# Another order of relu, finish and spectra steps in the final stage, and one prefetch load a unit earlier

## Chip, core and metric

The kernel runs on one core of a Trainium2 chip. The metric is the device time of one execution in microseconds (us); lower is better. The kernel before took 461.34 us, the median of 8 runs (459.61 to 462.4).

PE is TensorE, ACT or ScalarE the activation engine, DVE or VectorE the vector engine, POOL or GpSimd the general engine, SP or SyncE the queue that issues most DMAs. Each works through its own queue in program order and waits on semaphores. PE writes its results to PSUM; GpSimd's adds here read and write SBUF alone.

## What is computed

Sliding-window attention with a bias that falls with distance makes x; then the first 64 Fourier modes of x along the sequence are multiplied by complex weight matrices, one pair per mode, transformed back and added to x; the sum goes through one dense layer with a relu.

```
q, k, v: 8 batches x 8 heads x 576 tokens x 64     x = attention, 8 x 576 x 512
X = rfft(x, axis=1)[:, :64]
Yr = Xr @ w_r - Xi @ w_i;  Yi = Xr @ w_i + Xi @ w_r      (per mode, 512 x 512 float32)
y = irfft(Y, n=576)
u = x + y
out = u + max(u @ w_ch, 0)
```

## The kernel before

**Attention.** Sixteen units, one for each batch and each half of the heads, go through a software pipeline. Its order is written out by hand in `STAGE` (step name, tile, lag in units). The order of instructions on every engine, SP among them, is that of the program: no scheduler moves any. `norm` (L348) writes a unit's x; SP loads q, k and v two units ahead (L208 to L220).

**Weights.** There are 128 weight matrices of 512 x 512 float32, 1 MB each. `load_w` fetches one either by SP (L453, kept as float32, the upper halves used as bf16) or by GpSimd (L449, the DMA converts to bf16). During attention, GpSimd fetches the first ones into the 14 buffers of pool `early`. The table `AHEAD` says after which pipeline stage how many loads are issued: `13: 4` means four after stage 13. Ahead of them GpSimd copies one element of the x of unit stage-1 into a gate tile (L520). This holds the load back until that unit is normalized. `LATER` adds three loads after each of stages 14 and 15. After attention, eight more GpSimd loads reuse early buffers, and SP streams the others through six, later eight, float32 buffers.

**Weight stage.** For each group of four modes, L648 multiplies the spectra XC with the weights into `acc`. Beside it, `early_spectra` and `project` prepare what the first 32 modes and x give: `project` leaves x @ w_ch and the first half of the modes' share of it in `XW` (L629). After the last group, `quad_end` moves the result into YT (L541 to L553), and the final stage starts.

**Final stage.** The output is cut into 18 units j: units 0 to 3 are the four token tiles of batches 0 and 1, 4 to 7 those of batches 2 and 3, 8 the last 64 tokens of these four batches; 9 to 12, 13 to 16 and 17 are the same for batches 4 to 7. Four pairs of batches bp need a spectra step each.

- `spectra(1, bp, ...)`, called for bp = 0 directly and by `late_spectra` (steps s1 to s3) for the others: four L566 matmuls give zw, four L569 matmuls give z, into a yy buffer; ACT copies zw to `ZW` (L571); z goes to `Z` in two copies (L573), on ACT for s1 to s3 and on DVE for bp = 0.
- `activate(j)` (step a): L712 matmuls bring XW into an mm buffer, L587 matmuls add the second half of the modes from ZW, ACT writes the relu to r (L731). For j in `POOLED`, GpSimd then adds x to r (L733).
- `finish(j)` (step f): for j not in `POOLED`, two L739 matmuls bring x into a yy buffer; L752 matmuls (L758 for units 8 and 17) add y = FT.T @ Z; DVE adds yy and r into o (L766); SP writes o out (L768, or L776 for units 8 and 17).

mm and yy have two PSUM buffers each, r has four buffers in SBUF, o five. A unit's mm is free when its relu is done, its yy when DVE's add is done, a spectra step's yy when its copies are done. The order of steps is a string written out by hand:

```python
        begin(0)
        add_tokens(0)
        spectra(1, 0, pair("yy")[:, 0], pair("mm")[:, 0], nc.vector.tensor_copy)
        for step in ("a0 f0 a1 a2 f1 s1 a3 a4 f2 f3 a5 a6 f4 f5 s2 a7 a8 f6 f7 a9 a10 f8 f9 s3 "
                     "a11 a12 f10 f11 a13 a14 f12 f13 a15 a16 f14 f15 a17 f16 f17").split():
```

`add_tokens(0)` ahead of the loop takes the first yy buffer for unit 0, and f0 gives it back.

Of the kernel before, what the change touches and what calls it, by code (L numbers as in the profile page):

```python
# [397 lines left out]
def kernel(  # L398
# [10 lines left out]
    nc = tc.nc  # L409
    ctx.enter_context(tc.manual_schedule(engines=ALL | {SP}))  # L410
    B, H, S, _ = q.shape
    NM, DM, _ = moe_w_r.shape
    AHEAD = {0: 1, 1: 1, 2: 1, 4: 1, 5: 1, 7: 1, 8: 1, 10: 1, 11: 1, 13: 4, 14: 1}
    LATER = {14: 3, 15: 3}
    EARLY, NWA, NWB, AGAIN = 14, 6, 2, 8
    HM = NM // 2
# [23 lines left out]
    def load_w(n, pool, bf16, chosen=None):  # L440


        for i in ([i for i in todo_w if i not in again][:n] if chosen is None else chosen):
            todo_w.remove(i)
            src = (moe_w_r, moe_w_i)[i % 2][i // 2].rearrange("(p a) e -> p a e", a=4)
            homes[i] = pool
            if bf16:
                t = spare.pop(0) if pool is None else pool.tile([P, 4, DM], BF16, tag="w", name="w")
                nc.gpsimd.dma_start(out=t, in_=src)  # L449
                wq[i] = [t[:, a] for a in range(4)]  # L450
            else:
                t = pool.tile([P, 4, DM], FP32, tag="w", name="w")
                nc.sync.dma_start(out=t, in_=src)  # L453
                wq[i] = [t[:, a].bitcast(BF16)[:, 1::2] for a in range(4)]

    with ExitStack() as actx:
# [51 lines left out]
        for stage in range(min(lags), n + max(lags)):  # L508
# [6 lines left out]
            if stage == 3:  # L515
                at.inverse_table()
            if stage in AHEAD:
                if stage:
                    b, g = at.units[stage - 1]
                    nc.gpsimd.tensor_copy(gate[:1, :1], x[:1, b, 0, 256 * g : 256 * g + 1])  # L520
                load_w(AHEAD[stage], early, True)
            if stage in LATER:
                load_w(LATER[stage], None, True)

    with ExitStack() as mctx:
# [35 lines left out]
        def spectra(hf, bp, zw, z, copy):  # L561

            lhsT = [YT[:, hf, et, 2 * bp : 2 * bp + 2].rearrange("p b r m -> p (b r m)")
                    for et in range(4)]
            for et in range(4):
                nc.tensor.matmul(zw, lhsT=lhsT[et], rhs=wch[:, et],  # L566
                                 start=(et == 0), stop=(et == 3))
            for et in range(4):
                nc.tensor.matmul(z[:, et * P : (et + 1) * P], lhsT=lhsT[et], rhs=ident,  # L569
                                 start=True, stop=True)  # L570
            nc.scalar.copy(ZW[:, bp, hf], zw)  # L571
            for i in range(2):
                copy(Z[ROWS[i], 2 * bp + (i if hf else 1 - i)], z[ROWS[i]])  # L573
# [24 lines left out]
        def token_tiles(j):  # L598
            b, st = units[j]
            return x[:, b : b + 2, st] if st < FULL else x[:, b + 1 : b + 4 : 2, FULL]  # L600
# [91 lines left out]
        pctx.close()  # L692
        wctx.close()

        fin = mctx.enter_context(tc.tile_pool(name="res", bufs=4, reuse_waits="tile"))
        ps = mctx.enter_context(
            tc.tile_pool(name="tps", bufs=2, space=PSUM, reuse_waits="tile")
        )
        POOLED = (2, 4, 6, 8, 10, 12, 14)
        mms, yys, rs = {}, {}, {}  # L700

        def pair(tag):
            return ps.tile([P, 2, DM], FP32, tag=tag, name=tag)
# [13 lines left out]
        def activate(j):  # L717
# [12 lines left out]
            for part in ((slice(0, 1), slice(1, 2)) if j == 0 else (slice(0, 2),)):  # L730
                nc.scalar.activation(r[:, part], mm[:, part], AF.Relu)  # L731
            if j in POOLED:
                nc.gpsimd.tensor_tensor(out=r, in0=r, in1=token_tiles(j), op=ALU.add)  # L733
# [8 lines left out]
        def finish(j):  # L742

            b, st = units[j]
            if j in POOLED:
                yys[j] = pair("yy")
# [3 lines left out]
            for n in range(2):  # L750
                if st < FULL:
                    nc.tensor.matmul(  # L752
                        yy[:, n], lhsT=FT[:, n, st * P : (st + 1) * P], rhs=Z[:, b + n],
                        start=j in POOLED, stop=True, skip_group_check=True,
                    )
                    continue
                for half in range(2):
                    nc.tensor.matmul(  # L758
                        yy[ROWS[half], n], lhsT=FT[:, half, FULL * P :],
                        rhs=Z[:, b + half + 2 * n],  # L760
                        start=j in POOLED, stop=True, skip_group_check=True,
                    )
# [17 lines left out]

        def late_spectra(bp):
            zz = pair("yy")
            spectra(1, bp, zz[:, 0], zz[:, 1], nc.scalar.copy)

        begin(0)
        add_tokens(0)
        spectra(1, 0, pair("yy")[:, 0], pair("mm")[:, 0], nc.vector.tensor_copy)
        for step in ("a0 f0 a1 a2 f1 s1 a3 a4 f2 f3 a5 a6 f4 f5 s2 a7 a8 f6 f7 a9 a10 f8 f9 s3 "
                     "a11 a12 f10 f11 a13 a14 f12 f13 a15 a16 f14 f15 a17 f16 f17").split():
            {"a": activate, "f": finish, "s": late_spectra}[step[0]](int(step[1:]))  # L790


# [28 lines left out]
```

## Time and profile before

| | us |
|---|---|
| median of 8 runs | 461.34 |
| the profiled execution, its own time | 461.3 |
| its span, first to last instruction | 459.2 |
| last weight matmul (L648) starts | 415.28 |
| first DVE add of the final stage (L766) starts | 420.74 |
| last DVE add ends | 454.32 |

Busy in the whole span: PE 363.1 us, DVE 171.8, ACT 155.5, POOL 51.8. From 418.8 to 454.4 us, most of the final stage: PE 27.7 us, DVE 22.9, ACT 22.6, POOL 14.8 of 35.6.

The page divides the span into forty slices with one digit of busy share for each engine; DMA there is the mean share of sixteen DMA engines, which can pass 1 by a little in the finer windows. In rows of instructions the first two numbers are the start in us and the length in us, x4 counts merged instructions, and square brackets tell how long the engine sat idle before and what ended it. In the chain of waits, "issue" is time in which nothing visible was waited for.

### The profile page before, as it was taken

How to read it: one execution, taken by the hardware profiler on the slowest of the kernel's cores; microseconds unless marked ns; L12 is line 12 of the kernel's file. 1: busy time of each engine (PE TensorE's matmuls, PEld its weight loads, DVE VectorE, ACT ScalarE, POOL GpSimd, SP SyncE). 2: the span in 40 equal slices, each digit the busy share in tenths (PEclk: the TensorE clock that was granted, in tenths of full speed). 3: DMA queues.
4: the chain of work that ended last, by engine and by line, in shares of the span. 5: the costliest groups of instructions: out<-in, count | busy, mean ns of one | idle time of the engine just before them, and what ended most of it. 6: DMA issues, size and time to landing. Idle time of an engine off the chain costs nothing. (4 is left out here: it accounts for less than half of the span.)

```text
span 459.2 us, 7797 instructions
## 1 busy us (share of the span) xinstructions
PE 363.1 (79%) x3271; PEld 191.2 (42%) x3294; DVE 171.8 (37%) x312; ACT 155.5 (34%) x193; POOL 51.8 (11%) x84
## 2 busy tenths in 40 slices
PE   5797999999875558656676798998989788988773
PEld 4466777777653222212222243443433333433331
DVE  7988799998722001000010142111111211203555
ACT  6878899999700000000000021211111111104761
POOL 8510101002310100000000000000000000001460
PEclk9999899999989575776666699999999999999998
DMA  8999999996999999999999999999999999991687
GB/s 284 323 338 308 291 292 307 329 289 179 214 310 317 281 314 317 345 398 425 417 422 422 422 420 420 418 422 420 420 420 422 418 420 420 421 378 49 230 274 274
DMA packets 51875, 158.31 MB, mean 345 GB/s; under 512 B 3713, under 2 KB 22657, under 8 KB 39041
## 3 DMA queue, kind: packets, MB, share of 16 engines
q1 hardware_dynamic: 47280, 142.62, 80.5%
q0 software_dynamic: 4560, 15.21, 16.7%
q8 instruction: 25, 0.41, 0.4%
q14 instruction: 10, 0.07, 0.0%
HBM read 163.58 MB, written 9.44 MB: 377 GB/s over the span
## 5 line engine op out<-in xcount | busy, mean ns | idle before, releaser
L648 PE MATMUL acc<-w,XC 128*32 128x512 bf16 x488 | 147.1, 458 | 50.2 <-DMA w<-in_moe_w_r_dram 27.2
L648 PEld LDWEIGHTS <-XC 128*32 128x32 bf16 x512 | 59.7, 140 | 130.6 <-issue 100.7
L295 ACT ACTIVATE att<-sc 128x1024 bf16<-128x1024 f32 x64 | 64.0, 1031 | 7.8 <-PE sc L285 7.8
L629 ACT CAST XW<-my 128x512 bf16<-128x512 f32 x36 | 21.1, 586 | 109.0 <-PE my L587 109.0
L571 ACT CAST ZW<-zw 128x512 bf16<-128x512 f32 x4 | 2.3, 586 | 138.6 <-PE zw L566 138.6
L543 DVE TENSOR_SCALAR yq<-acc 128x512 bf16<-128x512 f32 x14 | 9.7, 690 | 100.8 <-PE acc L648 100.8
L611 DVE COPY xT<-tr 128x1024 bf16<-128x1024 bf16 x18 | 12.5, 692 | 89.4 <-PE tr L609 89.4
L733 POOL TENSOR_TENSOR r<-r,x 128x1024 f32<-128x1024 f32 x7 | 14.8, 2129 | 273.3 <-ACT r L731 273.3
L332 PE MATMUL av<-vb,att 128*128 128x132 bf16 (+1 forms) x576 | 38.5, 217 | 4.7 <-DVE x L348 3.0
L332 PEld LDWEIGHTS <-att 128*128 128x128 bf16 x704 | 36.6, 98 | 10.3 <-DVE x L348 7.3
L623 PE MATMUL my<-wch,xT 128*64 128x512 bf16 x288 | 37.9, 385 | 0.8 <-DVE xT L611 0.8
L257 ACT COPY qkT<-tp 128x1152 bf16<-128x1152 bf16 x30 | 33.5, 1117 | 3.4 <-PE tp L251 2.6
L285 PE MATMUL sc<-qkT 64*64 64x256 bf16 (+2 forms) x640 | 25.9, 271 | 5.1 <-ACT qkT L257 1.2
L348 DVE TENSOR_TENSOR x<-av,rec 128x640 bf16<-128x640 f32 x32 | 26.4, 825 | 1.1
L766 DVE TENSOR_TENSOR o<-yy,r 128x1024 f32<-128x1024 f32 (+1 forms) x20 | 21.5, 1114 | 12.6 <-POOL r L733 6.6
L285 PEld LDWEIGHTS <-qkT 64*64 64x64 bf16 x640 | 14.9, 111 | 19.9 <-issue 16.9
L623 PEld LDWEIGHTS <-xT 128*64 128x64 bf16 x288 | 13.2, 109 | 22.6 <-issue 9.4
L234 DVE CAST vb<-vr 64x1024 bf16<-64x1024 f32 x32 | 22.2, 694 | 0.2
L306 DVE TENSOR_TENSOR att<-att,mask 128x1024 bf16<-128x1024 bf16 x32 | 20.6, 684 | 0.0
L731 ACT ACTIVATE r<-mm 128x1024 f32<-128x1024 f32 (+1 forms) x19 | 17.3, 981 | 4.0 <-PE mm L587 3.9
L272 PE MATMUL sc<-bias,ident 128*128 128x512 bf16 x48 | 17.1, 413 | 1.4 <-ACT att L295 1.4
L251 PE MATMUL tp<-ident,q 128*128 128x128 bf16 x144 | 12.0, 236 | 4.1 <-DVE q L239 4.1
(104 smaller groups left out, 329.8 us busy)
## 6 DMA issues: line engine op xcount, KB each, us to landing
w<-in_moe_w_i_dram SPq DMA_DIRECT2D x54, 1024.0 KB, 18.4
w<-in_moe_w_r_dram SPq DMA_DIRECT2D x46, 1024.0 KB, 18.5
qr<-in_q_dram SPq DMA_DIRECT2D x16, 576.0 KB, 9.0
kr<-in_k_dram SPq DMA_DIRECT2D x16, 576.0 KB, 8.2
vr<-in_v_dram SPq DMA_DIRECT2D x32, 256.0 KB, 7.2
w<-in_moe_w_r_dram POOLq DMA_DIRECT2D x15, 512.0 KB, 24.5
out_dram<-o SPq DMA_DIRECT2D x15, 512.0 KB, 3.1
w<-in_moe_w_i_dram POOLq DMA_DIRECT2D x7, 512.0 KB, 9.0
```

Source lines behind the costliest of these rows:

```text
L234: nc.vector.tensor_copy(self.vb[u % 2][row, :, :, :, W * half : W * half + D], src[row, :2])
L257: (self.nc.vector.tensor_copy if u < 2 and w == "q" else self.nc.scalar.copy)(dst.rearrange("q h (p j) -> q h p j", j=TPP), tp.rearrange(" ...
L285: nc.tensor.matmul(sc[64 * half : 64 * half + 64, e, j * 256 + c0 : j * 256 + c0 + n], lhsT=qkT[row, 1, h, k0 + j : k0 + P : 2], rhs=qkT[r ...
L295: self.nc.scalar.activation(self.att[u % 2][:, kt * 8 * P : (kt + 1) * 8 * P], sc.rearrange("p e n -> p (e n)"), AF.Exp, scale=1.0 / math. ...
L306: nc.vector.tensor_tensor(out=rows, in0=rows, in1=self.table[:, heads], op=ALU.mult)
L332: nc.tensor.matmul(bank[:, qt * W : qt * W + rhs[j].shape[1]], lhsT=att[:, o : o + P], rhs=rhs[j], start=(n == 0 and j == 0), stop=(n == l ...
L348: nc.vector.tensor_tensor(out=self.x[:, b, :, cs].rearrange("p t (h d) -> p h t d", h=2), in0=tiles[:, :, :, :D], in1=rec.unsqueeze(-1).br ...
L623: nc.tensor.matmul(mm[ROWS[half]], lhsT=lhsT, rhs=wch[:, dt], start=(dt == 0), stop=False, skip_group_check=True,)
L629: nc.scalar.copy(XW[:, j, n], mm)
L648: nc.tensor.matmul(acc[32 * (i // 2) : 32 * (i // 2) + 32], lhsT=XC[:, c0 : c0 + 31 * NM + 1 : NM], rhs=w[a], start=(ri == 0 and a == 0), ...
L731: nc.scalar.activation(r[:, part], mm[:, part], AF.Relu)
L766: nc.vector.tensor_tensor(out=o[:, c], in0=yy[:, c], in1=r[:, c], op=ALU.add)
```

## The change

```diff
-    AHEAD = {0: 1, 1: 1, 2: 1, 4: 1, 5: 1, 7: 1, 8: 1, 10: 1, 11: 1, 13: 4, 14: 1}
+    AHEAD = {0: 1, 1: 1, 2: 1, 4: 1, 5: 1, 7: 1, 8: 1, 10: 1, 11: 1, 12: 1, 13: 3, 14: 1}
...
-        fin = mctx.enter_context(tc.tile_pool(name="res", bufs=4, reuse_waits="tile"))
+        fin = mctx.enter_context(tc.tile_pool(name="res", bufs=6, reuse_waits="tile"))
...
-        POOLED = (2, 4, 6, 8, 10, 12, 14)
+        POOLED = (1, 4, 5, 6, 9, 10, 15, 16)
...
         def late_spectra(bp):
             zz = pair("yy")
-            spectra(1, bp, zz[:, 0], zz[:, 1], nc.scalar.copy)
+            spectra(1, bp, zz[:, 0], zz[:, 1], nc.vector.tensor_copy if bp == 1 else nc.scalar.copy)
...
-        for step in ("a0 f0 a1 a2 f1 s1 a3 a4 f2 f3 a5 a6 f4 f5 s2 a7 a8 f6 f7 a9 a10 f8 f9 s3 "
-                     "a11 a12 f10 f11 a13 a14 f12 f13 a15 a16 f14 f15 a17 f16 f17").split():
+        for step in ("a0 s1 a2 a1 f2 a4 s2 f0 f1 a7 a8 f4 a9 f7 f8 a5 a3 f9 f3 a12 a10 f5 s3 f12 "
+                     "a16 a14 f10 f14 a11 f16 a6 f11 a17 a15 f6 a13 f13 f15 f17").split():
```

The order of the steps is new: s1 comes straight after a0, s2 ahead of f0, units are no longer taken by number, and relus may run further ahead of their finishes, for which r gets two buffers more. GpSimd adds x for eight units instead of seven, and for other ones. The Z copies of s1 go from ScalarE to VectorE. One of the four GpSimd loads issued after stage 13 is issued after stage 12 instead, behind a gate copy of its own that reads the x of unit 11. The number of loads and their buffers stay.

## Prediction

> **What bounds the kernel now.** I read the page's forty slices first, then the windows by stage, then the chain of waits of the last 40 us, then the groups of the final stage.
>
> ```profile
> span 459.2 us, 7797 instructions
> ...
> DVE  7988799998722001000010142111111211203555
> ...
> DMA  8999999996999999999999999999999999991687
> ```
>
> A slice is 11.48 us. DMA is full from slice 10 to slice 34: the expert weights stream in, and the other engines wait. Two places are not full: slice 9 (103 to 115 us) and the final stage after about 412 us, where no engine is full (DVE 3 to 5 tenths). So two terms add: the length of the weight stream, and the final stage. The windows show the hole in slice 9; the column before the last is the DMA share.
>
> ```profile
> core 0: us, PE busy (x) PEld busy (x) DVE busy (x) ACT busy (x) POOL busy (x), PEclk, DMA share, GB/s
> ...
> 106.00:108.00 2.00, 1.82 (x41) 1.55 (x32) 1.95 (x5) 2.00 (x3) 0.00 (x0) 1.00 0.37 94
> 108.00:110.00 2.00, 1.68 (x33) 1.33 (x32) 1.94 (x5) 1.92 (x4) 0.00 (x0) 1.00 0.30 80
> 110.00:112.00 2.00, 2.00 (x38) 1.49 (x36) 1.34 (x3) 2.00 (x3) 1.73 (x4) 1.00 0.87 236
> 112.00:114.00 2.00, 1.89 (x41) 1.52 (x39) 1.55 (x3) 1.70 (x3) 0.84 (x2) 1.00 0.70 133
> 114.00:116.00 2.00, 1.57 (x30) 1.10 (x29) 1.92 (x5) 1.94 (x3) 0.00 (x0) 1.00 1.04 209
> ```
>
> Full is 1.04 here. Missing are 2 us x (0.67 + 0.74 + 0.17 + 0.34) = 3.8 us of DMA time, 2.8 of them before 110 us. GpSimd's timeline says why: after its load at 97.07 it sleeps 12.66 us until unit 12's x exists.
>
> ```profile
> 97.07 0.53 POOL L449 DMA_DIRECT2D w<-in_moe_w_r_dram  x1
> 110.27 0.51 POOL L520 COPY gate<-x 1x1 bf16<-1x1 bf16 x1 [12.66 <-DVE x L348]
> 110.72 0.53 POOL L449 DMA_DIRECT2D w<-in_moe_w_i_dram  x1
> ```
>
> The final stage is a loop of waits; the chain shows one turn:
>
> ```profile
> 425.40 1.95 ACT r L731 x2
> 427.35 0.07 issue
> 427.42 2.14 POOL r L733
> 429.56 0.03 issue
> 429.58 1.24 DVE o L766
> 430.82 0.04 issue
> 430.86 1.02 PE yy L566 x4
> ```
>
> Relu, GpSimd's add, VectorE's add; only then is a yy buffer free for the next spectra step, and the relus behind it need those spectra. The turn repeats at 439.27, 8.4 us later. DVE's rows from its first Z copy (418.81) to its last add (end 454.32) have 22.0 us of work and 13.5 of idling.
>
> **What the Trainium skill says.** "DMA: Bandwidth & Descriptors", section "Issuing engines are not separate DMA queues": loads of GpSimd and SyncE run on the same 16 DMA engines. The trace agrees: the share stays at 1.02 to 1.07 while both have loads out. Section "Anatomy of one DMA — SWDGE (gpsimd) path" gives a fixed cost of about 2.0 us. The trace: load issued 110.72, DMA full from about 113. "SBUF — State Buffer", section "Who interferes with whom": VectorE and GpSimd exclude each other when a VectorE instruction has two SBUF inputs, not with one. VectorE's final adds read yy from PSUM and r from SBUF; the trace agrees, GpSimd's add from 429.51 takes 2.13 us under a VectorE add, and 2.13 alone.
>
> **The change, part by part.**
>
> *1. One prefetch a unit earlier.* It adds one gate copy (L520, 0.5 us on an idle POOL) and moves one L449 load (0.53 us of POOL). The only other work behind them on POOL is stage 13's gate, 6 us later. Unit 12's normalization (DVE, 109.31) released the gate at 110.27; unit 11's stands at 102.72, so the load issues at 102.72 + 0.96 + 0.45 = 104.1 and moves data from about 106. Its price in DMA time: 0.524 MB written at 209 to 217 GB/s (rows where only such loads run) is 2.45 us; an SP weight load, 1.049 MB at 422 GB/s, is 2.49. The 2.8 us before 110 hold it. SP's v loads are the only transfers it can delay: that of 108.06 is cast at 119.61, and that of 101.46 at 113.42, at 7.2 us from issue to landing, so over 4 us of slack. At 110.7 three loads remain instead of four (7.4 us from 112.5, to 119.9); the next ones issue from 116.82, flowing about 118.9, so no new hole opens. From 120 to 400 us the weight loads issued and not yet landed always amount to more than 13 us of DMA time, so nothing after it runs dry, and the stream ends **2.45 us earlier**. Bounds: 1.3 if VectorE's work delays the load's descriptors by a microsecond and more; 2.6.
>
> *2. The final stage's order, eight POOL units, s1's Z copies on VectorE, six r buffers.* Counts: POOL 8 adds for 7 (+2.1 us), PE two L739 matmuls less (-0.43), VectorE two more Z copies of 0.71 (+1.42), ScalarE two fewer (-1.17). These are busy times; the end is set by waits, so I laid both orders out queue by queue, in program order, with this profile's durations. Start to start: relu of 1024 columns 0.92, GpSimd add 2.09, VectorE add 1.14 (half: 0.60), ZW copy 0.49, Z copy 0.59 on ScalarE and 0.71 on VectorE; PE groups L712 and L587 0.21 each (0.43 for the tail units 8 and 17), L739 and L752 0.43 each, L566 with L569 1.09, 0.1 more when the tile shape changes. A PE result is ready 0.39 after its last start; a hand-off costs 0.05 (POOL from ScalarE 0.085). Two mm and two yy buffers, five o. Both start at the last weight matmul's end, 415.67.
>
> The old order in this layout gives VectorE's last add an end of 454.20, against 454.32 in the trace, and no add's start differs by more than 0.2. The new order, VectorE's adds (us, and what each waited for):
>
> ```
> f2  423.88  its yy: s1's Z copies (DVE, to 422.75), then L739 and L752
> f0  426.98  s2 stands ahead of it on PE and waits for f2's add (425.11)
> f1  428.80  its yy: s2's Z copies on ScalarE, to 428.11
> f4  430.73  PE, behind the relu groups of units 7 and 8
> f7 432.25  f8 433.39  f9 434.75  f3 435.89  f5 437.27: near back to back
> f12 439.62  PE, behind s3's 1.1 us
> f10 441.15  f14 442.29  f16 443.48  f11 444.64: near back to back
> f6  446.96  GpSimd's add, ended 446.91
> f13 448.53  f15 449.82 (GpSimd, 449.78)  f17 451.01, 451.61; end 452.29
> ```
>
> yy of unit 0 stays taken until f0, so the first steps run through one yy buffer: VectorE's first add comes 3.3 us later than before (423.88 for 420.56). This is won back because s2's results come at 428.1 for 433.7 and s3's at 440.1 for 442.1, and because most GpSimd adds finish before VectorE asks for them. Idling falls from 13.4 to 10.1 us in the layouts, VectorE's work grows by 1.4: **1.9 us** earlier. SP issues an out transfer in 0.43 us and a tail unit's two in 1.3, under VectorE's pace on average; 9.44 MB in the 27 us from 425.1 needs 350 GB/s, where the trace's last windows moved up to 382; at 300 the five o buffers would hold VectorE 0.4 us. Six r buffers cost no time: they lie in space the weights have left. Behind the last add both orders have the same f17, so the 4.9 us to the span's end stay. Bounds: hand-offs of 0.15 instead of 0.05 leave 1.25, a PE switch longer by 0.2 leaves 0.9, hand-offs of 0 give 2.1. I keep 0.7 to 2.6, half a microsecond beyond for what the layout does not hold.
>
> Sum: -2.45 - 1.9 = -4.35. The profiled execution took 461.3 (span 459.2 and 2.1 around it), the median is 461.34: 457.0.
>
> **Rivals.** *The load is hidden anyway*: something other than DMA throughput sets the stream's end. For it, PE is 8 to 9 tenths busy from 390 to 413; against it, L648 waits for DMA to within 11 us of the end. Only the stage's 1.9: 459.4. *The order gains nothing*: the layout is tight where it has PE just in time (f4, f12, f13), and PE hand-offs longer by 0.2 each at nine such places eat 1.8. Only the load: 458.9. *Slower*: VectorE's denser adds shut GpSimd out of SBUF. If each of the eight adds (L733) took 3.8 us instead of 2.1, f9, f16, f6 and f15 would all wait for GpSimd and the layout ends at 458.0, 3.7 later than before; less 2.45, 462.6. The point of decision is about 3.5 us an add. Against it stand the 2.13 us under a VectorE add. *It does not do what it says*: if the new gate waited for unit 12, nothing moves in part 1: again 459.4.
>
> **How the numbers follow.** Forecast 457.0, chance 0.66, its own range 455.5 to 458.6. Order gains nothing, 458.9: 0.14. Load gains nothing, 459.4: 0.12. Slower, 462.6: 0.05; some mixture that cancels: 0.03. A measurement here tells 0.2% (0.9 us) from no change. The first three are faster: 0.92; same 0.03; slower 0.05. The range reaches from both gains at their upper bounds (5.2) less a scatter of 0.9 between runs, 455.2, to the single gains, 459.4, and 0.2 of scatter: 459.6.
>
> **What would show it.** A load issue at POOL near 104.1, DMA share near 1 from 106 to 109, the last L648 matmul at about 412.8 instead of 415.3, f2's add 8.2 us after it, VectorE's last add 36.6 us after that matmul's end instead of 38.65, and L733 still at 2.13. A last L648 at 415 breaks part 1; a stage over 38 us breaks part 2, and a longer L733 says by which rival.

## The result and the profile after

The changed kernel takes 456.9 us (median of 11 runs, 455.97 to 458.64) where the kernel before takes 461.06 (32 runs): the ratio is 0.9912, 95% interval 0.9893 to 0.9932, so 4.1 us faster by the ratio, 4.16 by the medians. The forecast was 457.0. A second series gave 456.52 against 460.69, ratio 0.9918 (0.9894 to 0.9942).

The profiled execution took 457.68 us with a span of 455.9. The slices of its page, to be held against those of before:

```profile
span 455.9 us, 7803 instructions
...
DVE  7989699998732101000010142111111111202684
...
DMA  8999999999999999999999999999999999990598
```

The dip of DMA in slice 9 is gone: that digit is 9 where it was 6. The windows resolve it (last but one column: DMA share, 1.04 is full):

```profile
106.00:108.00 2.00, 1.82 (x43) 1.56 (x33) 1.95 (x4) 2.00 (x3) 0.00 (x0) 1.00 1.13 238
108.00:110.00 2.00, 1.68 (x33) 1.33 (x32) 1.94 (x5) 1.93 (x4) 0.00 (x0) 1.00 0.98 208
110.00:112.00 2.00, 2.00 (x37) 1.49 (x36) 1.44 (x3) 2.00 (x3) 1.63 (x4) 1.00 0.90 246
112.00:114.00 2.00, 1.89 (x41) 1.52 (x39) 1.45 (x3) 1.70 (x2) 0.42 (x1) 1.00 1.02 178
```

Before, the same four windows stood at 0.37, 0.30, 0.87 and 0.70. GpSimd's timeline has the new gate and the moved load (start, length, and in brackets the sleep before):

```profile
103.77 0.57 POOL L520 COPY gate<-x 1x1 bf16<-1x1 bf16 x1 [6.07 <-DVE x L348]
104.29 0.53 POOL L449 DMA_DIRECT2D w<-in_moe_w_i_dram  x1
110.37 0.51 POOL L520 COPY gate<-x 1x1 bf16<-1x1 bf16 x1 [5.55 <-DVE x L348]
```

In the final stage VectorE's timeline shows where the waits now lie:

```profile
419.52 1.39 DVE L573 CAST Z<-yy 64x512 bf16<-64x512 f32 x2 [1.28 <-ACT ZW L571]
422.10 1.23 DVE L766 TENSOR_TENSOR o<-yy,r 128x1024 f32<-128x1024 f32 x1 [1.19 <-ACT r L731]
425.10 1.29 DVE L766 TENSOR_TENSOR o<-yy,r 128x512 f32<-128x512 f32 x2 [1.77 <-PE yy L752]
...
439.52 4.75 DVE L766 TENSOR_TENSOR o<-yy,r 128x1024 f32<-128x1024 f32 x4 [0.30 <-PE mm L587]
445.26 1.23 DVE L766 TENSOR_TENSOR o<-yy,r 128x1024 f32<-128x1024 f32 x1 [0.99 <-POOL r L733]
446.87 3.75 DVE L766 TENSOR_TENSOR o<-yy,r 128x1024 f32<-128x1024 f32 x4 [0.39 <-ACT r L731]
```

f2, f0, f12 (not shown) and f6 wait 1.0 to 1.8 us, where the layout has them waiting; most adds between them follow closely. Only one wait is for GpSimd (1.0 us), where four were (6.6 us). From the end of the last weight matmul (413.72) to VectorE's last add (450.63) it is 36.91 us, where it was 38.65.

### The profile page after: what moved, and what is told of

Same layout as the page of the kernel before. It is cut to its first block, busy times and chain, and to the rows that moved or that the text cites. A ratio compares the mean times of both kernels' runs of the same rounds, so it can differ in the third digit from the quotient of the medians.

```text
span 455.9 us, 7803 instructions
## 1 busy us (share of the span) xinstructions
PE 356.6 (78%) x3269; PEld 190.4 (42%) x3292; DVE 173.4 (38%) x314; ACT 154.7 (34%) x191; POOL 54.6 (12%) x86
## 4 chain that ended last, share of the span: by engine, by line
DMA 54%; PE 25%; DVE 12%; issue 3%; ACT 3%; POOL 1%; ACTq 0%; DVEq 0%; SPq 0%; POOLq 0%
DMA w<-in_moe_w_i_dram 33%; DMA w<-in_moe_w_r_dram 13%; DMA vr<-in_moe_w_i_dram 7%; PE acc L648 6%; PE av L332 4%; PE my L623 2%; DVE x L348 2%; DVE vb L234 2%; PE tp L251 2%; DMA qr<-in_q_dram 2%; DVE att L306 2%; DVE q L239 1%; PE xt L369 1%; DVE o L766 1%; PE warm L636 1%
## 5 line engine op out<-in xcount | busy, mean ns | idle before, releaser
L648 PE MATMUL acc<-w,XC 128*32 128x512 bf16 x488 | 142.7, 443 | 56.9 <-DMA w<-in_moe_w_r_dram 33.0
L648 PEld LDWEIGHTS <-XC 128*32 128x32 bf16 x512 | 60.0, 139 | 130.5 <-issue 98.3
L733 POOL TENSOR_TENSOR r<-r,x 128x1024 f32<-128x1024 f32 x8 | 17.1, 2132 | 273.7 <-ACT r L731 273.6
L520 POOL COPY gate<-x 1x1 bf16<-1x1 bf16 x11 | 5.8, 527 | 86.5 <-DVE x L348 86.5
```

The costliest lines, as they stand in the source:

```text
L648: nc.tensor.matmul(acc[32 * (i // 2) : 32 * (i // 2) + 32], lhsT=XC[:, c0 : c0 + 31 * NM + 1 : NM], rhs=w[a], start=(ri == 0 and a == 0), ...
```

## Experiments

Each kernel was timed in five rounds beside the kernel before, and profiled once. "Stage" is from the end of the last L648 matmul to the end of VectorE's last add, "tail" from there to the span's end. Stages of one order repeat to 0.01 us in every profile. Tails repeat less well (5.28 to 5.57 us in five profiles of the changed order), and the end of the weight stream wanders by over 3 us between executions (last L648 start at 411.2 to 414.6 in the twelve profiles that have an early load). So stages are read from one profile, and streams from medians.

**The two halves apart.** The load alone:

```diff
# kernel before
-    AHEAD = {0: 1, 1: 1, 2: 1, 4: 1, 5: 1, 7: 1, 8: 1, 10: 1, 11: 1, 13: 4, 14: 1}
+    AHEAD = {0: 1, 1: 1, 2: 1, 4: 1, 5: 1, 7: 1, 8: 1, 10: 1, 11: 1, 12: 1, 13: 3, 14: 1}
```

> Only the prefetch load moved, final stage as before. My theory (the load fills a hole in the DMA time, the weight stream ends earlier by one load, 2.45 us; 1.95 seen in the changed kernel's one profile): 2.0 to 2.5 us under the kernel before, about 458.8 where that takes 461.1, the last L648 matmul at 412.8 to 413.4, and the stage from that matmul's end to the last VectorE add unchanged at 38.6. Rival (the load was hidden anyway, the whole gain is the order's): within 0.5 us of the kernel before.

Measured: 459.04 against 461.36, ratio 0.9947 (0.9928 to 0.9966); stage 38.64, tail 4.89, both as before. The gain of 2.3 by the medians is the load's. The last L648 matmul started at 414.63 in the profile, not at the expected 412.8 to 413.4; that execution was the longest of this kernel's seven, 460.7, so it says little.

The order alone:

```diff
# changed kernel
-    AHEAD = {0: 1, 1: 1, 2: 1, 4: 1, 5: 1, 7: 1, 8: 1, 10: 1, 11: 1, 12: 1, 13: 3, 14: 1}
+    AHEAD = {0: 1, 1: 1, 2: 1, 4: 1, 5: 1, 7: 1, 8: 1, 10: 1, 11: 1, 13: 4, 14: 1}
```

> Only the final stage as in the changed kernel, four loads after stage 13 as before. My theory: the last L648 matmul stays at 415.3, the stage up to the last VectorE add takes 36.9 us instead of 38.65, the last writes land some 0.4 later behind it, so 1.3 to 1.9 us under the kernel before, and the two halves' gains add up to the whole change's 4.2. Rival (the new order pays only with the early load): no gain, or the two halves do not add up by over 1 us.

Measured: 459.49, ratio 0.9968 (0.9951 to 0.9985); stage 36.91, tail 5.30. That is 1.9 by the medians and 1.5 by the ratio; stage and tail together give 1.3. The last L648 matmul started at 414.24, not at the expected 415.3: without the early load too the stream's end wanders by a microsecond. The halves add up: 2.32 + 1.87 = 4.19. Neither needs the other.

**Is it the hole, or just an earlier load?** One more load is moved:

```diff
# changed kernel
-    AHEAD = {0: 1, 1: 1, 2: 1, 4: 1, 5: 1, 7: 1, 8: 1, 10: 1, 11: 1, 12: 1, 13: 3, 14: 1}
+    AHEAD = {0: 1, 1: 1, 2: 1, 4: 1, 5: 1, 7: 1, 8: 1, 10: 1, 11: 1, 12: 2, 13: 2, 14: 1}
```

> The changed kernel with two loads after stage 12 and two after stage 13. The hole between 106 and 114 us now has 0.6 us of free DMA time left of 3.8 (shares 0.98, 0.90, 1.02 against 1.04). If the gain of the moved load is the filled hole, a second one finds little: 0.2 to 0.6 us under the changed kernel at most. Rival (each load issued earlier by a unit is worth about 2 us, whatever the hole): 454.9. A loss would mean that SP's v loads or VectorE's casts are now late.

Measured: 456.73, ratio 0.9906 (0.9888 to 0.9923), which the changed kernel's 0.9912 is not told from. The windows from 106 to 114 us stand at 1.13, 1.05, 1.08 and 1.11: the hole is full. In this kernel a load issued earlier is worth what it finds idle, not a fixed 2 us.

**What delays VectorE's first adds.** PE's timeline of the changed kernel:

```profile
420.97 0.61 PE L739 MATMUL yy<-x,ident 128*128 128x512 bf16 x2 [1.11 <-DVE Z L573]
421.42 0.59 PE L752 MATMUL yy<-Z,FT 128*128 128x512 bf16 x2
423.38 1.02 PE L566 MATMUL yy<-wch,YT 128*128 128x512 bf16 x3 [0.81 <-DVE o L766]
```

The first two rows are f2's: they wait until s1's Z copies give back the yy buffer, and end at 422.01. f2's relu had ended at 421.42, so its add at 422.10 waits for these matmuls, though the bracket above names the relu. The third row is s2's, which waits for f2's add. The test:

```diff
# changed kernel
         begin(0)
-        add_tokens(0)
         spectra(1, 0, pair("yy")[:, 0], pair("mm")[:, 0], nc.vector.tensor_copy)
```

> The changed kernel without the call add_tokens(0) ahead of the loop: unit 0 takes its yy buffer when f0 comes, so s1, f2, s2 have two yy buffers instead of one. If the yy buffer held for unit 0 is what delays the first VectorE adds (my reading: f2 at 8.4 us after the last weight matmul, f0 at 11.4 behind s2), s2's matmuls no longer wait for f2's add, and the layout, done again for this order, ends 2.1 us earlier: 454.8 where the changed kernel takes 456.9, stage about 34.8. Rival (VectorE's adds, GpSimd and PE hand-offs set the length, and the first wait is made up later anyway): within 0.5 us of the changed kernel, or slower by the 0.43 us of PE time that the two L739 matmuls now cost in the loop.

Measured: 454.56, ratio 0.9856 (0.9835 to 0.9878), from four executions; stage 34.74. VectorE's timeline:

```profile
418.05 1.39 DVE L573 CAST Z<-yy 64x512 bf16<-64x512 f32 x2 [1.28 <-ACT ZW L571]
419.47 1.23 DVE L766 TENSOR_TENSOR o<-yy,r 128x1024 f32<-128x1024 f32 x1
422.00 1.29 DVE L766 TENSOR_TENSOR o<-yy,r 128x512 f32<-128x512 f32 x2 [1.30 <-PE yy L752]
```

f2's add now follows s1's Z copies without a wait and comes 1.3 us earlier in the stage; two units later the gain is 2.17 us, and it stays to the end of the stage. So the yy buffer that unit 0 held, while s1, f2 and s2 shared the other one, cost 2.17 us of stage, the largest loss left in the new order that a run here removes. A second series:

> The changed kernel without the early add_tokens(0), once more, beside its further variants: stage 34.7 us, about 2.0 under the changed kernel, 6.3 under the kernel before.

455.51 against 461.06, ratio 0.9876 (0.9843 to 0.9909), stage 34.74, tail 5.95 where the first series had 5.30.

**The other parts of the order.** Beside them ran the changed kernel itself:

> The changed kernel once more, beside its variants: 456.9 (4.2 under the kernel before), stage from the last weight matmul's end to the last VectorE add 36.9 us.

456.52, stage 36.91. The Z copies of s1 back on ScalarE:

```diff
# changed kernel, in late_spectra
-            spectra(1, bp, zz[:, 0], zz[:, 1], nc.vector.tensor_copy if bp == 1 else nc.scalar.copy)
+            spectra(1, bp, zz[:, 0], zz[:, 1], nc.scalar.copy)
```

> The changed kernel with s1's two Z copies back on ScalarE. If VectorE's two extra copies (1.4 us) are worth it because ScalarE is relieved, as the move suggests, putting them back costs up to 1 us. The layout says the opposite: ScalarE is idle then, VectorE's first add waits for these copies either way, and the stage ends 0.4 us earlier: 36.5 us, 456.5 in all, which a timing can hardly tell and the profile can.

456.50; stage 36.54. The move to VectorE costs 0.37 us of stage, a small part of the change that works against it; the times (ratio 0.9914 for 0.9918) do not tell the two apart. Four r buffers:

```diff
# changed kernel
-        fin = mctx.enter_context(tc.tile_pool(name="res", bufs=6, reuse_waits="tile"))
+        fin = mctx.enter_context(tc.tile_pool(name="res", bufs=4, reuse_waits="tile"))
```

> The changed kernel with four r buffers instead of six. If relus that run ahead need six, a relu waits for VectorE's add of four units before, and the stage is longer by 0.5 us or more. The layout finds no relu that waits for an r buffer with four: stage 36.9, the same time.

456.95, ratio 0.9919 (0.9900 to 0.9937), stage 36.91: the two buffers do nothing.

**GpSimd's units.**

```diff
# changed kernel
-        POOLED = (1, 4, 5, 6, 9, 10, 15, 16)
+        POOLED = (2, 4, 6, 8, 10, 12, 14)
```

> The new order with GpSimd adding x for the seven units of before (2, 4, 6, 8, 10, 12, 14). My theory: which units go to GpSimd belongs to the order; f2, first in the new order, would now wait 2.1 us for GpSimd, and units 1, 9, 15 and 16 hold a yy buffer through two more PE groups. The layout ends 3.7 us later: stage 40.6, 460.6 in all, most of the order's gain and more lost. Rival (the order of steps alone carries the gain, the set of units hardly matters): within 0.5 us of the changed kernel.

Measured: 460.50 (fourteen executions, 458.58 to 466.56), ratio to the kernel before 1.0005 (0.9982 to 1.0028). The new order needs its own set of units; with the old set the whole gain is gone, the early load's too. (The old order with the new set was not run.) The median is as laid out, but the stage of the profiled execution, which took 463.26, was 42.63 us, 2 more than laid out. The windows (the number ahead of the DMA share is the clock granted to PE):

```profile
420.00:422.00 2.00, 0.96 (x10) 0.26 (x10) 0.97 (x2) 1.49 (x2) 1.34 (x1) 1.00 0.00 0
422.00:424.00 2.00, 0.21 (x4) 0.10 (x1) 1.19 (x1) 1.02 (x1) 1.42 (x2) 1.00 0.00 0
424.00:426.00 2.00, 1.91 (x9) 1.05 (x9) 0.04 (x1) 0.00 (x0) 1.48 (x1) 0.63 0.52 198
426.00:428.00 2.00, 1.11 (x3) 0.26 (x2) 1.13 (x2) 1.64 (x3) 0.00 (x0) 0.50 0.17 65
428.00:430.00 2.00, 2.00 (x12) 0.54 (x12) 0.48 (x2) 0.00 (x0) 0.00 (x0) 0.50 0.70 262
```

PE is busy for 1.17 of the 4 us from 420; then its clock stands at 0.5 for 6.8 us (424.5 to 431.4), and a 512-column matmul comes every 0.43 us instead of every 0.216. The run with filler matmuls tests whether the idling did this:

```diff
# the kernel of the last run
+        def fill(n):
+            t = pair("mm")
+            for _ in range(n):
+                nc.tensor.matmul(t[:, 0], lhsT=ident, rhs=XW[:, 0, 0], start=True, stop=True)
...
-        for step in ("a0 s1 a2 a1 f2 a4 s2 f0 ...
+        for step in ("a0 s1 a2 a1 f2 a4 w9 s2 f0 ...
```

> The new order with GpSimd's units of before, and nine matmuls of 512 columns (1.9 us, their result is read by nothing) into a free mm buffer ahead of s2. The run before had a stage of 42.6 us where the layout gave 40.6 (36.6 for the changed kernel, plus 3.7 and 0.3 of the layout's usual shortfall): PE's matmuls took twice their time from 424.5 to 431.4, with a granted clock of 0.5, right after PE had stood idle. If the idling before s2 brought the clock down, the filler keeps it at 1.0 and the stage takes 40.3 to 40.9; if the clock falls for another reason, the stage stays at 42.6 or more.

Its windows keep the clock, and the stage takes 40.31 us, 2.3 less:

```profile
422.00:424.00 2.00, 1.95 (x10) 0.88 (x9) 1.23 (x1) 0.60 (x1) 1.42 (x2) 1.00 0.00 0
424.00:426.00 2.00, 1.09 (x8) 0.52 (x7) 0.88 (x2) 1.30 (x3) 0.80 (x1) 1.00 0.70 262
```

That is what was expected if the idling brought the clock down, and the other expectation, 42.6 or more, did not come; it is one profile of each kernel. The timed ratio is 0.9980 (0.9963 to 0.9997) for 1.0005 without the filler, some 1.2 us less, with intervals that meet. Timing alone does not show the filler's gain, and whether every execution has the slow stretch stays open.

**A version beyond both.** With two yy buffers free from the start, a few moves in the order (four steps change place, not six as the expectation counts) and, in the last run, the second early load:

```diff
# changed kernel without the early add_tokens(0)
-        for step in ("a0 s1 a2 a1 f2 a4 s2 f0 f1 a7 a8 f4 a9 f7 f8 a5 a3 f9 f3 a12 a10 f5 s3 f12 "
-                     "a16 a14 f10 f14 a11 f16 a6 f11 a17 a15 f6 a13 f13 f15 f17").split():
+        for step in ("a0 s1 a2 a1 f2 a4 f0 s2 f1 a7 a8 f4 a9 f7 f8 a5 a3 f9 f3 a10 f5 a12 s3 f12 "
+                     "a16 a14 f10 f14 a11 f16 a6 a15 f11 a17 a13 f6 f13 f15 f17").split():
```

> Without the early add_tokens(0), and with six moves in the order that the layout favours, now that two yy buffers are free: f0 ahead of s2, a10 and f5 ahead of a12, a15 ahead of f11, a13 ahead of f6. The layout ends 0.75 earlier than without these moves: stage 34.0, about 0.5 under late0 after what the writes take back. If the writes to DRAM now set the end, nothing is gained though the stage is shorter, and the tail from the last VectorE add to the end grows from 5.3 by as much.

454.84, ratio 0.9856 (0.9820 to 0.9892); stage 33.87, tail 5.67, which lies between the 5.30 and 5.95 without the moves, so these profiles do not show whether the writes take the moves' gain back.

> best_order with two loads after stage 12 and two after stage 13: by the run with that split alone (0.2 under the changed kernel, not told from zero), 0 to 0.4 under best_order.

455.18, ratio 0.9860 (0.9827 to 0.9892); stage 33.87, tail 5.81. The stage is 0.87 shorter than without the moves; in time neither is told from the 0.9876 without them. By the ratios these versions are 2 to 3 us faster than the changed kernel, and dropping the early `add_tokens(0)` is what does most of it (0.9856 and 0.9876 in its two series).

## Why the prediction was right

*The load.* Predicted: issue at 104.1, DMA near 1 from 106 to 109, 2.45 us. Measured: 104.29, shares 1.13 and 0.98, 2.3 us by the medians of the load alone, interval 1.6 to 3.3. "The load is hidden anyway" and "it does not do what it says" fall with that run. The sign "last L648 at about 412.8" cannot be read from single profiles: it started at 415.28 and 414.24 in the two without the early load, and at 411.21 to 414.63, median 413.05, in the twelve with one. The prediction adds 2 us from issue to data and sets the skill's fixed cost of about 2.0 us beside them. That section of the Trainium skill, "Anatomy of one DMA — SWDGE (gpsimd) path" in "DMA: Bandwidth & Descriptors", puts most of this cost behind the last byte, so the 2 us rest on the trace alone: issued at 104.29, and from 106 the share is 1.13 where it was 0.37.

*The stage.* Predicted from the layout: f2's add at 8.2 us after the last weight matmul's end, last add ending at 36.6, VectorE's idling down by 3.3 us. Measured: 8.39, 36.91, and idling from 35.51 - 22.89 = 12.62 to 33.78 - 24.51 = 9.27 us, from the first Z copy of the stage to the last add. (The prediction's 22.0 us of work and 13.5 of idling match a count from start to start, without the overlap of neighbouring instructions; by busy time they are 22.89 and 12.62.) The layout falls short by 0.1 us in the old order and by 0.3 in the new one, and it named the first wait rightly, as the run without the early yy buffer shows (laid out -2.1, measured -2.17). "The order gains nothing" falls with the run of the order alone.

*The slower rival.* GpSimd's adds take 2.12 to 2.14 us in every profile, however dense VectorE's adds are. The Trainium skill, "SBUF — State Buffer", section "Who interferes with whom", says that a VectorE instruction with at most one SBUF input, outside the two-port modes, does not contend with GpSimd; VectorE's adds, with yy in PSUM and r in SBUF, bear it out here.

*The term that was mis-sized* is the tail, costed at no change because f17 is last in both orders. It grew from 4.88 to 5.28 us in the changed kernel and to 5.30 in the order alone. The windows near the end, first those of before:

```profile
446.00:448.00 2.00, 1.55 (x20) 0.66 (x19) 1.58 (x2) 1.15 (x3) 2.00 (x2) 1.00 0.63 240
448.00:450.00 2.00, 1.46 (x8) 0.43 (x8) 1.96 (x3) 0.80 (x1) 0.47 (x1) 1.00 0.72 268
```

and those of the changed kernel:

```profile
446.00:448.00 2.00, 1.08 (x5) 0.39 (x4) 1.61 (x2) 0.84 (x1) 2.00 (x1) 1.00 1.01 377
448.00:450.00 2.00, 1.14 (x6) 0.24 (x5) 1.94 (x4) 0.00 (x0) 0.13 (x1) 1.00 0.98 368
```

The writes keep DMA full from 440 to 452 us in the changed kernel; before, it was full from 450 to 456 only, after the gap shown. The median time from issue to landing of a 512 KB write rose from 3.1 to 3.9 us. SP's rows show where the tail grew, f17's four writes before and in the changed kernel:

```profile
453.75 2.45 SPq L776 DMA_DIRECT2D out_dram<-o  x4
```

```profile
450.06 2.83 SPq L776 DMA_DIRECT2D out_dram<-o  x4
```

Both start 0.57 us before VectorE's last add ends. Issuing them takes 0.38 us longer, nearly all of the tail's 0.40; the last of them lands 2.4 us after its issue in both. So it was SP's issue that took longer, behind writes that were slower to land. That the full DMA engines hold SP up fits this, but no run here separates it.

The prediction compared the mean rate needed (350 GB/s) with the highest seen (382), and not the rate at the end. With the tail the stage is worth 1.74 - 0.40 = 1.3 us in the profile, not 1.9; the medians' 1.9 for the order alone is within its interval of 0.7 to 2.3, so the sum's closeness to 4.35 is in part luck.

## What to carry to other kernels

Add a transfer's price only where the windows show DMA idle, and only as much as they show: one load filled most of the hole, and a second one's gain could not be told from none. In a stage of waits, lay the order out queue by queue with the profile's own durations and look first for a buffer that is taken long before it is used; giving that one back gained as much as the whole reordering. Then check what follows the stage: when adds come closer together, the writes behind them come closer together too, and here that took 0.4 of 1.74 us back.

## What the runs showed of the hardware

PE's granted clock fell to half for 6.8 us though no pause of PE near it was longer than 1.9 us: two pauses, of 1.1 and 1.9 us, between 419.9 and 424.1 us went ahead of it in the kernel with the old set of units. In the changed kernel, pauses of 1.1, 0.8 and 1.3 us between 419.9 and 426.4 us left it at 1.0. The Trainium skill, "TensorE: Matmul & The Clock Gate", section "HAM oscillation — how this bites in real kernels", states the rule as no idle gap over some 3.4 us; the run here fits shorter gaps close together doing it too.

The clock records of the fourteen traces say more: every stretch at one clock, except the last of each trace, lasts a whole multiple of 3.413 us. Call such 3.413 us a slot. In the slot that ends with the fall above, 421.12 to 424.53 us, PE was busy for 1.53 us, 45%; in the final stage of the changed kernel's profile, no slot up to 448.8 us has less than 62%. Over all fourteen traces, from 30 us on, 163 slots at full clock were followed by half clock, with PE busy for at most 53% of each, and 1262 by full clock, with PE busy for at least 45%. So in these traces the clock falls after a slot in which PE was busy for less than about half, and where the pauses lie in the slots counts beside their length.
